# An adaLN attention and MLP block on one core: modulation raws asked for earlier, first MLP weights split earlier, raw tokens kept in SBUF, LayerNorm transposes in the products' bank rotation

## The chip, the cores and the metric

The kernel runs on one core of a Trainium2 chip. The metric is the device time of one execution in microseconds, the median of several runs. The engines are called as in the profile: PE is TensorE, DVE is VectorE, ACT is ScalarE, POOL is GpSimd, SP is SyncE, which here only issues DMAs.

## The reference

One transformer block for 2048 tokens of width D = 576, conditioned on a vector c.

```python
mod = (silu(c) @ w_mod).reshape(6, 576)          # sa, ca, ga, sb, cb, gb
h = layernorm(x) * (1 + ca) + sa
x = x + ga * attention(h)                        # 32 query heads on 16 cached kv heads, head width 128,
                                                 # only the last 512 of the 2048 cached keys, softmax, @ wo
h = layernorm(x) * (1 + cb) + sb
gate, up = h @ W_gate, h @ W_up                  # F = 4608
x = x + gb * ((where(gate > 0, gate, 0) * up) @ W_down)
```

## The kernel before

All matrix products are made in fp32r with operands split into a high and a low part (hi, lo), and a product is three matmuls: hi x hi, hi x lo, lo x hi.

Attention runs in 128 **units**; a unit is one kv group, one block of 512 queries and one of the two heads. On the engines a unit is: scores s (PE, L446 to L448), their row maxima (DVE, L451 to L466), spread over partitions by two small matmuls with the constant quad (PE, L474), mask mb and scaled scores p (DVE, L521), exponentials (ACT, L523), hi (ACT, L510) and lo (POOL, L530), row sums ks (half on DVE, L536, half on POOL, L539), the product with v (pv, PE, L548 to L550), the next unit's queries (qps, PE, L374; qhi on ACT, qlo on DVE, L430) and a piece of the output projection (wo, PE, L575, added up through ACT, L584 and L608). In a unit all these stages belong to different units of a software pipeline.

After the units comes the gated **MLP**. The gate and up products of a pair of F tiles with a half of the tokens are made by a Strassen-like scheme of seven products P1, P6, P2, P7, P5, P4, P3 (gu, L915); P2 is added up in the bank pair of P1 and P3 in that of P5. There are 18 pairs for each of two token halves, m = 0 to 35. After a product, DVE and ACT gate it (L936 to L965), ACT and POOL split the result into hhi (L930) and hlo (L931), and md matmuls (L575) multiply it by W_down; DVE adds md to acc (L586). The operands of the seven products are sums of parts of the tokens (names B11, B21, B22, T1 to T4, h in the code) and of the weights (wop, wk). The sums are made once: `h0_comb` and `h0_cut` make the token operands of the first half from SBUF tiles h0, `h_later(1, ...)` those of the second half, `w_later` the weight operands of the first pair from DRAM. Each such item is a load (begin), one or more combinations (comb), a split into hi and lo (cut) and stores into DRAM (hkeep, wkeep), from which they are loaded when the MLP needs them.

PSUM has a pool psS with two double banks, psW with one, and px["x"] with one in the MLP. In the MLP the gate/up products take psS, psS, x in turn, and md takes psW.

The order of the instructions on PE, DVE, ACT and POOL is written out by hand, and kept. Work that does not belong to the steady pipeline is placed by a table: `step(name, t, fn)` runs fn at t = 10 * unit + position. A unit has four hooks at the positions 0, 4, 6 and 9, and `prep(name, t, pr, gap)` runs the compute part at hook t and issues its load gap hooks earlier. SP's order is that in which the loads are issued; a load waits on SP for its buffer. In the MLP `mat(m, s, fn)` places fn after product s of pair m. `prep_mod(j, t)` loads a raw slab wm of w_mod for row j (L136) into pool xp's tag xm (three buffers, which the ks tiles use too), and multiplies it onto macc (DVE, L126, L128); five slabs make a row; `mod_col(j)` turns it into a column with five small matmuls (mps, L165).

The second LayerNorm is made in two places. `norm_steps("b0"/"b1", ...)` makes token blocks 0 and 1 during the last units; the transposes are ltb (L317), the affine parts lfb (ACT L331, DVE L329), and they are stored as hb in DRAM and loaded again as h0. `ln_half` makes blocks 2 and 3 in the MLP, in pairs m = 2, 4, 6, 8: stats, norm, and three groups of transposes (ltlh, L897) with their affine (lflh, ACT, L900).

```python
        def trans(ds):
            ps = psW.tile([P, 2, 512], F32, tag="w", name=f"lt{nm}_{ds[0]}")
...
    for i in range(4):
        for s, fn in enumerate(ln_half(2 + i // 2, i % 2)):
            mat(2 + 2 * i, s, fn)
```

H in the table is 1070, ten times the number of unit 107.

Of the kernel before, what the change touches and what calls it, by code (L numbers as in the profile page):

```python
# [14 lines left out]
P = 128  # L15
# [18 lines left out]
def kernel(  # L34
# [215 lines left out]

    pend, pend_act = [], []
# [8 lines left out]
    class LayerNorm:  # L260
# [59 lines left out]
        def affine(self, ds, pool, tag, engs):  # L320
            qb = self.qb
            if self.key == "b":
                add, mul = mods["b"]
                for d, e in zip(ds, engs):
# [7 lines left out]
                    hb_store(qb, d, slice(0, 512), f[:n], nc.scalar)  # L332
# [417 lines left out]
    def h_later(b, s, t):  # L750
# [3 lines left out]
        eng = nc.vector if b else nc.gpsimd  # L754
# [15 lines left out]
        def comb(i):  # L770
            x, y = st["a"][:n], st["b"][:n]
            eng.tensor_tensor(x, x, y, op=ALU.add if terms[i][0] == "+" else ALU.subtract)
# [17 lines left out]
        return [begin] + ([cut] if len(terms) == 1 else [lambda i=i: comb(i) for i in range(1, len(terms))])  # L790

    h0 = {}
# [5 lines left out]
    def h0_comb(dst, a, b, t, op):  # L798
        n = 96 if t == 2 else P
        nc.vector.tensor_tensor(h0[(*dst, t)][:n], h0[(*a, t)][:n], h0[(*b, t)][:n], op=op)  # L800
# [22 lines left out]
    def w_later(s, xx, where):  # L823
# [14 lines left out]
        def comb(i):  # L838
            x, y = st["a"], st["b"]
            eng.tensor_tensor(x, x, y, op=ALU.add if terms[i][0] == "+" else ALU.subtract)  # L840
            if i + 1 < len(terms):
                get(st["b"], *terms[i + 1][1:])
            else:
                cut()
# [11 lines left out]
        return [begin] + ([cut] if len(terms) == 1 else [lambda i=i: comb(i) for i in range(1, len(terms))])  # L856

    def ln_half(qb, hh):
# [28 lines left out]
        def trans(ds):  # L887
            ps = psW.tile([P, 2, 512], F32, tag="w", name=f"lt{nm}_{ds[0]}")
            ps = ps.rearrange("p a (b n) -> p (a b) n", b=2)
# [3 lines left out]
            else:  # L893
                f = hp.tile([P, 2, 256], F32, tag="hT", name=f"lf{nm}_{ds[0]}")
# [9 lines left out]
        return [stats, norm, lambda: trans((0, 1)), lambda: trans((2, 3)), lambda: trans((4,))]  # L904
# [39 lines left out]

    def new_pair(m, s):
        i = npair[0]
        npair[0] += 1
        if i % 3 == 2:
            pair[m, s] = px["x"].tile([P, 2, 512], F32, tag="x", name=f"gu{i}")
        else:  # L950
            pair[m, s] = psS.tile([P, 2, 512], F32, tag="s", name=f"gu{i}")
# [146 lines left out]
    for t in range(5):  # L1098
# [11 lines left out]
               (H + 39, H + 39, H + 49, H + 49), (H + 51, H + 61, H + 71), (H + 51, H + 61, H + 71), www)  # L1110
    norm_steps("b1", 1, "b", None, None, (H + 34, H + 37, H + 40, H + 47), H + 48,
               (H + 59, H + 59, H + 69, H + 69), (H + 81, H + 91, H + 101), (H + 81, H + 91, H + 101), www)
# [122 lines left out]
    def then(fn):  # L1235
        def go():
            flush_stores(2)
# [3 lines left out]
    t = 952  # L1241
    items = [(s, xx) for s in ("P1", "P2", "P4", "P7", "P5", "P6", "P3") for xx in range(2)]
    for n, (s, xx) in enumerate(items):
        here = n < 7
        for fn in w_later(s, xx, (xp, "xm", 640) if here else (hp, "hT", 512)):
            step("w.l", t, fn if here else then(fn))
            t += 5 if here else 4
        if here:
            step("w.e", t + 3, flush_stores)
            t = t + 5 if n < 6 else 1062  # L1250
    step("w.e", t + 6, flush_stores)
    t0 = H + 74
    for t in range(3):
        step("h0.l", t0, h0_load, 0, 0, t)
        step("h0.l", t0, h0_load, 1, 0, t)
    cuts = [("B11", (0, 0), t) for t in range(3)] + [("B21", (1, 0), t) for t in range(3)]
    for n, c in enumerate(cuts):
        step("h0.c", t0 + 4 + 4 * n, then(lambda c=c: h0_cut(*c)))
    t0 = H + 104
    seq = []  # L1260
    for t in range(3):
        step("h0.l", t0 + 4 * t, h0_load, 1, 1, t)
        step("h0.l", t0 + 4 * t, h0_load, 0, 1, t)
        seq += [(h0_cut, "B22", (1, 1), t), (h0_comb, (1, 1), (1, 1), (0, 1), t, ALU.subtract),
                (h0_cut, "T3", (1, 1), t), (h0_comb, (1, 1), (1, 1), (0, 0), t, ALU.add),
                (h0_cut, "T2", (1, 1), t)]
    for t in range(3):
        seq += [(h0_comb, (0, 1), (0, 1), (0, 0), t, ALU.subtract), (h0_cut, "T1", (0, 1), t),
                (h0_comb, (1, 0), (1, 0), (1, 1), t, ALU.subtract), (h0_cut, "T4", (1, 0), t)]
    for n, c in enumerate(seq):  # L1270
        step("h0.s", t0 + 6 + 3 * n, then(lambda c=c: c[0](*c[1:])))
    step("h0.e", t0 + 9 + 3 * len(seq), flush_stores)
# [34 lines left out]
    for u in range(NU):  # L1307
# [108 lines left out]
```

## Time and profile before

| | |
|---|---|
| times of three runs | 3138.55, 3129.92, 3129.11 us; median 3129.92 |
| profiled execution | 3133.55 us; span 3131.8, mean granted PE clock 0.974 |
| matmuls and weight loads on PE | 15414 each, PE busy 2949.8 us |
| DMA | 435.82 MB, mean 139 GB/s |
| units 0 to 127 | from about 44 to 1766 us of the span |
| MLP pairs m = 0 to 35 | from about 1766 us to the end |

The page's first part gives the busy time of each engine. A windows view gives the same for chosen stretches, with the clock that PE was granted (1.00 is full). A waits view gives, for an engine and a line, what released it: total wait, how often, the longest. A line view gives the count of instructions, their busy time, mean duration in ns, and the idle time just before them.

### The profile page before, as it was taken

What the parts mean: (1) busy time and instruction counts of PE and PEld (TensorE: products, weight loads), DVE (VectorE), ACT (ScalarE), POOL (GpSimd) and SP (SyncE); (2) the same over time, 40 slices, a digit from 0 to 9 for tenths busy, and PEclk for the clock granted to TensorE, in tenths of its full rate; (3) what the DMA queues carried; (4) which work ended last, traced back from release to release, by engine and by line L of the source; (5) the groups of instructions that cost most, each with busy time, mean ns of one, the idle gap of its engine ahead of it and who ended that gap; (6) DMA issues with size and microseconds to landing.
All of it is one profiled execution on the core that took longest, in us unless ns stands there. A gap on an engine that the chain in (4) does not pass through costs nothing. (4 is left out here: it accounts for less than half of the span.)

```text
span 3131.8 us, 41177 instructions
## 1 busy us (share of the span) xinstructions
PE 2949.8 (94%) x15414; PEld 2544.4 (81%) x15414; DVE 2102.8 (67%) x2925; ACT 1369.8 (44%) x1885; POOL 1848.4 (59%) x1294
## 2 busy tenths in 40 slices
PE   6799999999999999998889988899989999999999
PEld 4688877877888888887777777778778888888888
DVE  7888877877888888776677555556676544444444
ACT  4466665656666666665555333332323211111110
POOL 5578877877788887777677555556666411111111
PEclk8899999999999999999999999999999999999999
DMA  4011122222212203232344555556777954444453
GB/s 143 23 60 52 47 91 80 82 88 91 82 58 81 65 31 107 85 131 80 127 160 146 180 213 212 198 209 234 259 266 261 335 178 173 159 162 165 166 172 113
DMA packets 173447, 435.82 MB, mean 139 GB/s; under 512 B 16128, under 2 KB 62976, under 8 KB 173248
## 3 DMA queue, kind: packets, MB, share of 16 engines
q1 hardware_dynamic: 131344, 291.36, 28.5%
q10 hardware_dynamic: 41904, 141.84, 11.6%
q8 instruction: 122, 2.00, 0.3%
q14 instruction: 77, 0.63, 0.1%
HBM read 283.71 MB, written 177.73 MB: 147 GB/s over the span
## 5 line engine op out<-in xcount | busy, mean ns | idle before, releaser
L530 POOL TENSOR_TENSOR lo<-p,hi 128x1024 fp32r<-128x1024 f32 x256 | 612.6, 2415 | 1.2 <-ACT hi L510 0.9
L539 POOL TENSOR_TENSOR ks<-ks,p 128x512 f32<-128x512 f32 x256 | 343.0, 1340 | 340.0 <-ACT p L523 302.6
L575 PE MATMUL md<-wogb,hhi 128*128 128x288 f32 x2304 | 479.1, 300 | 51.9 <-ACT lflh L900 32.1
L915 PE MATMUL gu<-hop_T,wop 128*128 128x512 f32 (+1 forms) x2016 | 500.5, 393 | 0.0
L586 DVE TENSOR_TENSOR acc<-md,acc 128x576 f32<-128x576 f32 x288 | 217.6, 755 | 420.0 <-PE md L575 419.9
L575 PEld LDWEIGHTS md<-wogb,hhi 128*128 128x128 f32 x2304 | 391.4, 192 | 82.6 <-ACT lflh L900 37.3
L915 PEld LDWEIGHTS gu<-hop_T,wop 128*128 128x128 f32 (+1 forms) x2016 | 369.2, 188 | 67.9
L915 PE MATMUL gu<-hop_B,wop 128*128 128x512 f32 (+1 forms) x1512 | 382.6, 396 | 3.7 <-DMA wop<-wk_P 2.8
L451 DVE TRANSPOSE_TENSOR_REDUCE t<-s 128x32 f32<-128x1024 f32 x256 | 314.8, 1240 | 103.7 <-PE s L448 94.1
L575 PE MATMUL md<-wogb,hlo 128*128 128x288 f32 x1152 | 345.1, 300 | 2.3 <-POOL hlo L931 2.3
L931 POOL TENSOR_TENSOR hlo<-r,hhi 128x512 fp32r<-128x512 f32 x72 | 98.9, 1374 | 408.9 <-issue 242.4
L915 PEld LDWEIGHTS gu<-hop_B,wop 128*128 128x128 f32 (+1 forms) x1512 | 282.0, 191 | 60.6 <-DMA wop<-wk_P 3.3
L374 PE MATMUL qps<-hTa,wA 128*128 128x512 f32 x1288 | 311.8, 393 | 8.5 <-ACT lfa L356 5.2
L575 PE MATMUL wo<-woga,ohi 128*128 128x288 f32 x1472 | 305.9, 300 | 2.3 <-DVE lfa L354 1.6
L374 PEld LDWEIGHTS qps<-hTa,wA 128*128 128x128 f32 x1288 | 244.2, 190 | 61.8 <-ACT lfa L356 5.6
L521 DVE TENSOR_TENSOR p<-s,mb 128x1024 f32<-128x1024 f32 x242 | 285.4, 1218 | 3.4
L523 ACT ACTIVATE p<-p 128x1024 f32<-128x1024 f32 x242 | 255.6, 1056 | 41.9 <-DVE p L521 35.6
L510 ACT CAST hi<-p 128x1024 fp32r<-128x1024 f32 x256 | 268.6, 1049 | 7.0
L575 PEld LDWEIGHTS wo<-woga,ohi 128*128 128x128 f32 x1472 | 238.6, 188 | 10.1 <-issue 2.0
L930 ACT CAST hhi<-r 128x512 fp32r<-128x512 f32 x72 | 44.7, 621 | 431.8 <-DVE r L940 368.3
L426 ACT ACTIVATE qhi<-qps 128x512 fp32r<-128x512 f32 x128 | 76.4, 597 | 350.5 <-PE qps L374 340.5
L575 PEld LDWEIGHTS md<-wogb,hlo 128*128 128x128 f32 x1152 | 220.9, 192 | 3.0 <-POOL hlo L931 3.0
(198 smaller groups left out, 5952.0 us busy)
## 6 DMA issues: line engine op xcount, KB each, us to landing
wop<-wk_P SPq DMA_DIRECT2D x133, 640.0 KB
wk_P<-wop ACTq DMA_DIRECT2D x119, 640.0 KB
wr<-wlay SPq DMA_DIRECT2D x68, 384.0 KB
dk<-wogb ACTq DMA_DIRECT2D x36, 576.0 KB
wogb<-dk SPq DMA_DIRECT2D x36, 576.0 KB
againq<-akq SPq DMA_DIRECT2D x18, 640.0 KB
rogb<-wd SPq DMA_DIRECT2D x36, 288.0 KB
rwA<-wq SPq DMA_DIRECT2D x32, 320.0 KB
```

Of the source, the lines that this page charges most:

```text
L374: return [lambda i=i, a=a, b=b: nc.tensor.matmul(ps, a, b, start=(i == 0), stop=(i == n - 1)) for i, (a, b) in enumerate(ops)]
L426: nc.scalar.activation(qhi[u], qst[u][0], AF.Copy, bias=0.0, scale=SCALE)
L451: nc.vector.tensor_reduce(t4[u][:, 2 * h:2 * h + 2, :].rearrange("p k b -> p (k b)"), t.rearrange("p k (b j) -> p (k b) j", j=32), axis=AX ...
L510: nc.scalar.copy(hi_[u, h], pt[u, h])
L521: nc.vector.tensor_tensor(p, t, bc[u][:, None, :].to_broadcast([P, 2, 512]), op=ALU.subtract)
L523: nc.scalar.activation(p, p, AF.Exp, bias=0.0, scale=1.0)
L530: nc.gpsimd.tensor_sub(lo_[u, h], pt[u, h], hi_[u, h].bitcast(F32))
L539: nc.gpsimd.tensor_tensor(ks_[u], ks_[u], p[:, j, :], op=ALU.add)
L575: nc.tensor.matmul(ps[:, half, :H2], a[:, sl], w[b][:, cs], start=(n == 0 and seed is None), stop=(n == 5), skip_group_check=seed is not None)
L586: nc.vector.tensor_tensor(av, ps[:, :, :H2], av, op=ALU.add)
L915: nc.tensor.matmul(ps, a, c, start=s not in ("P2", "P3") and i == 0, stop=i == len(ops) - 1, skip_group_check=True)
L931: nc.gpsimd.tensor_sub(lo, r, hi.bitcast(F32))
```

## The change

1. Modulation raws: the 15 slabs stand at t = 109 + 30 i instead of 104 + 50 i, and are asked for five hooks ahead instead of two. The columns m3.col and m4.col move from 310 and 560 to 230 and 380. The last row, macc5, is stored in DRAM at 536 and loaded back at 936, ahead of its use at 949, which stays.
2. The first MLP weights' operands (14 items of `w_later`) move from t = 952 and after (seven in the xm buffers, seven in the buffers hT) to units 55 to 90, all in xm. A comb and its cut, one step before, are two steps, 6 apart.
3. The affine results of blocks 0 and 1 are kept as h0 in SBUF for four of five column groups; eight stores (ACT) and eight loads (SP) fall away. The fifth group's two halves are stored by SP at H + 86 and H + 116 and loaded. The subtractions (DVE) and cuts (ACT, POOL) have a new table: cuts at positions 1 and 2 of a unit, subtractions at position 8. Operands' stores go out on SP instead of ACT, with four instead of two left waiting. Normalising and transposes of b0 and b1 move by up to a unit.
4. `ln_half`: stats run in the pair before, at its sixth product, and there are two groups of transposes instead of three: the last 64 columns after product 1, the other 512 after product 5. They take their PSUM from the rotation of the gate/up products (`new_banks`) instead of psW, and their affine result goes to a buffer of pool wC.
5. `h_later(1, ...)`: the combinations run on POOL instead of DVE, cut is a step of its own, and the operands B11 and B21 move to m = 5 to 8.
6. In each unit, `ksum_op` stands after `sum_bc` and `q_lo` instead of ahead of them.

```diff
-                    hb_store(qb, d, slice(0, 512), f[:n], nc.scalar)
+                    if d < 4:
+                        h0[d // 2, qb, d % 2] = f
+                    else:
+                        late.append(lambda f=f: hb_store(qb, 4, slice(0, 512), f[:64]))
...
-    def flush_stores(left=0):
+    def flush_stores(left=0, eng=None):
         while len(stores) > left:
             dst, src = stores.pop(0)
-            nc.scalar.dma_start(dst.bitcast(F32), src.bitcast(F32))
+            (eng or nc.scalar).dma_start(dst.bitcast(F32), src.bitcast(F32))
...
-        eng = nc.vector if b else nc.gpsimd
...
-            eng.tensor_tensor(x, x, y, op=ALU.add if terms[i][0] == "+" else ALU.subtract)
+            nc.gpsimd.tensor_tensor(x, x, y, op=ALU.add if terms[i][0] == "+" else ALU.subtract)
             if i + 1 < len(terms):
                 get(st["b"], *terms[i + 1][1:])
-            else:
-                cut()
...
         def trans(ds):
-            ps = psW.tile([P, 2, 512], F32, tag="w", name=f"lt{nm}_{ds[0]}")
+            ps = new_banks(f"lt{nm}_{ds[0]}").rearrange("p a (b n) -> p (a b) n", b=2)
...
-                f = hp.tile([P, 2, 256], F32, tag="hT", name=f"lf{nm}_{ds[0]}")
+                f = wp.tile([P, 4, 256], F32, tag="wC", name=f"lf{nm}_0")
...
-        return [stats, norm, lambda: trans((0, 1)), lambda: trans((2, 3)), lambda: trans((4,))]
+        return [stats, norm, lambda: trans((4,)), lambda: trans((0, 1, 2, 3))]
...
+    def new_banks(nm):
+        npair[0] += 1
+        pool, tag = (px["x"], "x") if npair[0] % 3 == 0 else (psS, "s")
+        return pool.tile([P, 2, 512], F32, tag=tag, name=nm)
...
-        prep(f"m{3 + i // 5}.{i % 5}", 104 + 50 * i, prep_mod(3 + i // 5, i % 5))
-    step("m3.col", 310, setd(mods, "b0", lambda: mod_col(3, 0.0)()))
-    step("m4.col", 560, setd(mods, "b", lambda: (mods["b0"], mod_col(4, 1.0)())))
+        prep(f"m{3 + i // 5}.{i % 5}", 109 + 30 * i, prep_mod(3 + i // 5, i % 5), 5)
+    step("m3.col", 230, setd(mods, "b0", lambda: mod_col(3, 0.0)()))
+    step("m4.col", 380, setd(mods, "b", lambda: (mods["b0"], mod_col(4, 1.0)())))
...
     for i in range(4):
-        for s, fn in enumerate(ln_half(2 + i // 2, i % 2)):
-            mat(2 + 2 * i, s, fn)
-    later = [fn for s in TERMS for t in range(3) for fn in h_later(1, s, t)]
-    for i, fn in enumerate(later):
+        m = 2 + 2 * i
+        for at_, fn in zip(((m - 1, 5), (m, 0), (m, 1), (m, 5)), ln_half(2 + i // 2, i % 2)):
+            mat(*at_, fn)
+    later = {s: [fn for t in range(3) for fn in h_later(1, s, t)] for s in TERMS}
+    for i, fn in enumerate(later.pop("B11") + later.pop("B21")):
+        mat(5 + i // 3, (0, 2, 4)[i % 3], fn)
+    for i, fn in enumerate(sum(later.values(), [])):
         mat(9 + i // 7, i % 7, fn)
...
-            flush_stores(2)
+            flush_stores(4, nc.sync)
...
-    t = 952
...
+    t = 546
+    for s in ("P1", "P2", "P4", "P7", "P5", "P6", "P3"):
+        for xx in range(2):
+            for fn in w_later(s, xx, (xp, "xm", 640)):
+                step("w.l", t, fn)
+                t += 6
             step("w.e", t + 3, flush_stores)
-            t = t + 5 if n < 6 else 1062
+            t += 6
+    assert t < 930, t
...
         exp_half(u, 1)
-        ksum_op(u, 0)
-        ksum_op(u, 1)
         if u:
             sum_bc(u - 1)
         if u + 1 < NU:
             q_lo(u + 1)
+        ksum_op(u, 0)
+        ksum_op(u, 1)
```

The order on the engines shows the moves at three places. First PE in pair m = 2 of the MLP (ltlh is a transposes' bank, gu a gate/up product's, md the down product's). Before, the transposes stand behind a finished product, and md comes seven matmuls later:

```order
L915 MATMUL gu_17631<-hop_B_2_16570,wop_17626 128x512
L897 MATMUL ltlh_0_0_17786<-ident,xnlh_0_0_17737 128x128
L897 MATMUL ltlh_0_0_17786<-ident,xnlh_0_1_17739 128x128
L915 MATMUL gu_17798<-hop_T_0_16826,wop_17677 128x512 x2
L915 MATMUL gu_17798<-hop_T_3_16829,wop_17677 128x512
L915 MATMUL gu_17798<-hop_T_1_16827,wop_17677 128x512 x2
L915 MATMUL gu_17798<-hop_T_4_16830,wop_17677 128x512
L915 MATMUL gu_17798<-hop_T_2_16828,wop_17677 128x512
L575 MATMUL md_1_0_17806<-wogb_17453,hhi_01_17622 128x288 x2
```

Now the first group there has 64 rows and stands one product earlier, and the others come together four products later:

```order
L916 MATMUL gu_17686<-hop_T_2_16531,wop_17566 128x512
L898 MATMUL ltlh_0_4_17721<-ident,xnlh_0_0_17681 64x128
L898 MATMUL ltlh_0_4_17721<-ident,xnlh_0_1_17683 64x128
L916 MATMUL gu_17625<-hop_B_0_16557,wop_17620 128x512 x2
L916 MATMUL gu_17625<-hop_B_3_16560,wop_17620 128x512
L916 MATMUL gu_17625<-hop_B_1_16558,wop_17620 128x512 x2
L916 MATMUL gu_17625<-hop_B_4_16561,wop_17620 128x512
L916 MATMUL gu_17625<-hop_B_2_16559,wop_17620 128x512
L579 MATMUL md_0_3_17736<-wogb_17433,hhi_00_17423 128x288 x2
```

The neighbours have the same shapes in both; moved are the place of the transposes and the bank that they hold while md comes.

Second, DVE in unit 120 (p are the scaled scores, ks the sums, qlo the next queries' low part, rb the output's scale, h or lfb the raw tokens h0). Before:

```order
L504 STREAM_TRANSPOSE mb_15961<-r_15957 128x512
L800 TENSOR_TENSOR h_111_15622<-h_111_15622,h_001_15138 128x512
L521 TENSOR_TENSOR p_0_15990<-s_0_15915,mb_15961 128x1024
L521 TENSOR_TENSOR p_1_15995<-s_1_15924,mb_15961 128x1024
L536 TENSOR_TENSOR ks_15998<-p_0_15990 128x512
L484 STREAM_TRANSPOSE rb_16002<-ri_15959 128x512
L430 SCALAR_TENSOR_TENSOR qlo_16004<-qps_15941,qhi_15963 128x512
L556 TENSOR_TENSOR rb_16002<-pv_15980,rb_16002 128x512
L451 TENSOR_REDUCE t_121_16052<-s_0_16045 128x32
```

After:

```order
L508 STREAM_TRANSPOSE mb_15932<-r_15928 128x512
L525 TENSOR_TENSOR p_0_15958<-s_0_15878,mb_15932 128x1024
L525 TENSOR_TENSOR p_1_15963<-s_1_15887,mb_15932 128x1024
L488 STREAM_TRANSPOSE rb_15966<-ri_15930 128x512
L434 SCALAR_TENSOR_TENSOR qlo_15968<-qps_15906,qhi_15934 128x512
L540 TENSOR_TENSOR ks_15970<-p_0_15958 128x512
L560 TENSOR_TENSOR rb_15966<-pv_15948,rb_15966 128x512
L804 TENSOR_TENSOR lfb_2_15487<-lfb_2_15487,lfb_0_14942 128x512
L804 TENSOR_TENSOR lfb_3_15489<-lfb_3_15489,lfb_1_14944 128x512
L804 TENSOR_TENSOR lfb_0_15353<-lfb_0_15353,lfb_0_14942 128x512
L804 TENSOR_TENSOR lfb_1_15355<-lfb_1_15355,lfb_1_14944 128x512
L455 TENSOR_REDUCE t_121_16015<-s_0_16008 128x32
```

The subtraction has left its place ahead of p, four stand in a row at the unit's end, and ks has gone behind qlo.

Third, the combinations of `h_later` in the MLP (hx is the operand in the making, acc the sum of md, hlo the low part that md needs, wop weights' operands). Before they stand on DVE, in the first pairs that have several terms, between the acc additions:

```order
L772 TENSOR_TENSOR hx_T_0_20618<-hx_T_0_20618 128x512
L586 TENSOR_TENSOR acc_125<-md_0_0_20672,acc_125 128x576
L586 TENSOR_TENSOR acc_126<-md_0_1_20693,acc_126 128x576
L730 TENSOR_TENSOR wr_01_20516<-wr_01_20516,wr_00_20379 128x768
L772 TENSOR_TENSOR hx_T_0_20618<-hx_T_0_20618 128x512
L586 TENSOR_TENSOR acc_127<-md_0_2_20735,acc_127 128x576
```

Now they stand on POOL, between hlo and the weights:

```order
L775 TENSOR_TENSOR hx_T_0_20063<-hx_T_0_20063 128x512
L932 TENSOR_TENSOR hlo_00_20137<-r_20133,hhi_00_20136 128x512
L695 TENSOR_TENSOR wop_20140<-wr_11_19803,wop_20140 32x2x128
L696 TENSOR_TENSOR wop_20140<-wr_11_19803,wop_20140 128x2x256
L177 TENSOR_TENSOR wogb_20146<-rogb_20061,wogb_20146 128x576
L775 TENSOR_TENSOR hx_T_0_20063<-hx_T_0_20063 128x512
L695 TENSOR_TENSOR wop_20184<-wr_01_19848,wop_20184 32x2x128
```

The number of matmuls is the same in both programs.

More of the change, by code (lines that the diff above doesn't have):

```diff
@@ L249, in hb_load @@
             nc.sync.dma_start(dst[:96], hb[qb, 4][j].rearrange("r p n -> (r p) n"))
+    h0, late = {}, []
     pend, pend_act = [], []
@@ L788, in cut @@
             stores.append((hkeep[b, s, t], hi[:n]))
-        return [begin] + ([cut] if len(terms) == 1 else [lambda i=i: comb(i) for i in range(1, len(terms))])
-    h0 = {}
+        return [begin] + [lambda i=i: comb(i) for i in range(1, len(terms))] + [cut]
+    H0_COMB = {"t3": ((1, 1), (1, 1), (0, 1), ALU.subtract), "t2": ((1, 1), (1, 1), (0, 0), ALU.add),
+               "t1": ((0, 1), (0, 1), (0, 0), ALU.subtract), "t4": ((1, 0), (1, 0), (1, 1), ALU.subtract)}
+    H0_CUT = {"B11": (0, 0), "B21": (1, 0), "B22": (1, 1), "T3": (1, 1), "T2": (1, 1), "T1": (0, 1),
+              "T4": (1, 0)}
     def h0_load(j, k, t):
@@ L854, in cut @@
             stores.append((wkeep[0, s][:, xx, 3:5, :].rearrange("p t n -> p (t n)"), lo))
-        return [begin] + ([cut] if len(terms) == 1 else [lambda i=i: comb(i) for i in range(1, len(terms))])
+        return [begin] + [lambda i=i: comb(i) for i in range(1, len(terms))] + [cut]
     def ln_half(qb, hh):
@@ L1251 @@
[L1251 to L1272, printed above, removed]
+    t = 546
[4 more added lines that the diff above has]
+                t += 6
+            step("w.e", t + 3, flush_stores)
+            t += 6
@@ L1273 @@
+    assert t < 930, t
+    for key, t, at_ in [(("l", 0, 0), 2, 96), (("l", 1, 0), 2, 96), (("l", 1, 1), 2, 122), (("l", 0, 1), 2, 122),
[7 rows of a table added]
+        if key[0] == "l":
+            step("h0.l", H + at_, h0_load, *key[1:], t)
+        elif key in H0_COMB:
+            step("h0.a", H + at_, h0_comb, *H0_COMB[key], t)
+        else:
+            step("h0.c", H + at_, then(lambda key=key, t=t: h0_cut(key, H0_CUT[key], t)))
+    step("h0.e", H + 181, flush_stores, 0, nc.sync)
     for t, s in ((1236, "B11"), (1246, "T2"), (1247, "B21"), (1266, "T3"), (1267, "T1"), (1276, "T4"),
```

31 lines of the change are left out of this document (12 added, 19 removed), and 7 rows, old and new, of the table t.

## The prediction

> **What bounds the kernel now.** I read the page's busy shares first, then windows laid over single units and single MLP pairs, then the waits inside the long ones, then the tiles and lines that the change moves.
>
> ```profile
> PE 2949.8 (94%) x15414; PEld 2544.4 (81%) x15414; DVE 2102.8 (67%) x2925; ACT 1369.8 (44%) x1885; POOL 1848.4 (59%) x1294
> ```
>
> TensorE (PE) is the bound and the others have room, so only time in which PE idles or runs slowly can be won. In the next fence each window is one unit, from its spread matmuls (L474) to the next unit's; or one or several pairs m of the MLP; the columns are PE, weight loads, DVE, ACT, POOL, granted clock, DMA share, GB/s.
>
> ```profile
> 453.60:476.80 23.20, 16.24 (x76) 13.97 (x75) 11.24 (x17) 7.68 (x10) 13.10 (x8) 0.78 0.21 70
> 476.80:488.90 12.10, 12.10 (x66) 10.57 (x65) 9.44 (x14) 8.77 (x12) 6.83 (x5) 1.00 0.22 71
> 526.50:547.10 20.60, 15.05 (x64) 12.34 (x65) 11.35 (x16) 8.73 (x12) 11.46 (x8) 0.83 0.33 111
> 658.40:677.70 19.30, 14.84 (x65) 11.95 (x65) 10.15 (x15) 8.83 (x12) 11.48 (x7) 0.82 0.33 117
> 726.20:745.60 19.40, 14.66 (x66) 11.99 (x65) 11.65 (x16) 7.68 (x10) 13.06 (x8) 0.82 0.34 119
> 794.70:813.60 18.90, 16.59 (x75) 13.96 (x74) 13.01 (x17) 8.83 (x12) 14.78 (x9) 0.82 0.21 69
> 1439.80:1748.60 308.80, 267.66 (x1316) 224.20 (x1314) 217.56 (x328) 173.52 (x241) 224.91 (x155) 0.94 0.43 142
> 1812.60:1847.90 35.30, 35.30 (x196) 31.21 (x195) 24.08 (x34) 12.33 (x17) 24.21 (x24) 1.00 0.61 221
> 1847.90:1894.70 46.80, 38.79 (x205) 33.41 (x204) 22.87 (x28) 12.97 (x20) 22.00 (x20) 0.96 0.55 193
> ...
> 2094.00:2140.60 46.60, 38.56 (x206) 33.27 (x204) 22.86 (x28) 13.48 (x21) 22.96 (x21) 0.96 0.57 199
> 2140.60:2419.60 279.00, 257.81 (x1359) 223.23 (x1358) 189.68 (x211) 85.15 (x125) 182.86 (x160) 0.97 0.75 263
> 1040.00:1366.00 326.00, 325.10 (x1707) 280.11 (x1706) 264.00 (x382) 214.62 (x286) 256.78 (x157) 1.00 0.24 79
> ```
>
> An undisturbed unit takes 12.1 us, an undisturbed pair 35.3. Against these floors there are four pools of lost time. A: units 30, 35, 45, 50, 55, together 101.4, less 5 x 12.1, is 40.9. B: the 20 units from 107 on, 308.8 less 242, is 66.8. C: pairs m = 2, 4, 6, 8 (first and last shown, 186.8 in all) less 141.2, is 45.6. D: seven pairs from m = 9, 279.0 less 247.1, is 31.9. Between 1040 and 1366 PE is 99.7% busy, so outside the pools little is left.
>
> **A: modulation raws.**
>
> ```profile
>   DMA wm<-wmod: 24.3, 4
> 450.33 5.47 SPq L136 DMA_DIRECT2D wm<-wmod  x1
> 461.83 0.82 DVE L128 SCALAR_TENSOR_TENSOR macc<-wm,sT,macc 128x576 f32<-128x576 f32 x1 [6.83 <-DMA wm<-wmod]
> DVE roga L217 <- DMA roga<-wo: 0.9, 1, 0.9
> SPq L136 <- DVE t L466: 18.3, 3, 6.6
> ```
>
> DVE waited 24.3 us in four waits for raws, and PE idles 101.4 - 77.4 = 24.0 in the five windows: the same microseconds, since the q_lo behind macc on DVE is what PE needs. The other 17 are half clock: 0.82 of 18.9 us is 3.4 lost. The raw of unit 30 was issued at 450.3, the issue alone took 5.5, and macc began only at 461.8: 11.5 later, and about 15 after the hook that asked for it (an estimate: one position of the unit more). There are four hooks to a unit of 12.1: two ahead are 6 us, five 15.7. Four waits should go. The m.col steps remain (now at units 23 and 38, directly behind the last raw's macc): unit 55 had no raw wait and still lost 6.8, so I leave 2 x 7. Gain 40.9 - 14 = 27 (18 if one or two raws stay late, 35 if the columns cost little). The parked macc5 is one store on ACT and one load on SP, the load a unit ahead of its use; by L136's 5.5 at most such an issue is nothing against the 24.3 that PE felt, and in the stretch of the load SP has room: 0 (to 5, if the load is late like a raw).
>
> **B: the last units.** Three things leave or spread here: 14 weight items, eight stores and eight loads of raw tokens, and the bunching of subtractions and cuts.
>
> ```profile
> ACT wb_P L849 <- POOL wa_P L840: 35.6, 7, 7.2
> PE qm L474 <- DVE t L466: 14.7, 5, 4.7
> PE wo L575 <- ACT wo L608: 14.6, 10, 4.1
> PE s L448 <- DVE qlo L430: 6.0, 6, 2.3
> DVE h L800 <- POOL hz_T L808: 7.0, 2, 3.5
> SPq L830 <- POOL wa_P L840: 58.3, 6, 19.1
> L800 DVE TENSOR_TENSOR h<-h,h 128x512 f32<-128x512 f32 x8 | 12.0, 1501 | 8.1 <-POOL hz_T L808 7.0 <-POOL hz_B L808 1.2
> L317 PE MATMUL ltb<-ident,xnb 128*128 128x128 f32 x32 | 4.1, 272 | 0.0
> L840 POOL TENSOR_TENSOR wa_P<-wa_P,wb_P 128x384 f32<-128x384 f32 x13 | 13.2, 1012 | 5.6 <-DMA wb_P<-wlay 3.0 <-DVE ri L479 2.5
> ```
>
> ACT stood 35.6 us for the weight combination in front of its own cut (both in one step), and PE's wait for the wo copy, 14.6, is ACT being late. That goes with the weights, as far as ACT caused it. DVE stood 7.0 for POOL inside a unit; with cuts and subtractions in different places of the unit that goes too. What stays: 40 LayerNorm transposes on PE (4.1 busy for 32, so 5), the LayerNorm's own DVE work, and 12 subtractions (h0). Four of them now stand in a row at the end of unit 120, three in 121: at 0.7 (L772's fastest, below) to 1.5 each, 2.8 to 6.0 us where DVE has (326 - 264) / 27 = 2.3 of room per unit. The sum of the pool: PE idle is 308.8 - 267.7 = 41.1, of which the three PE rows are 35.3; slow clock is 0.06 of 308.8, 18.5; transposes and the rest 7. Afterwards the wo wait leaves 2, the qm wait 8 (DVE's work is only spread), the s wait 3, the unnamed 6: idle 19, slow clock in the same ratio 9, transposes and the rest 7: 35 (20 to 50). Gain 66.8 - 35 = 32 (17 to 47). The 21 operand stores go from ACT to SP, flushed with four left; an SP store holds what is queued behind it until POOL's cut has ended. Before, SP stood 58.3 us for POOL in this stretch and PE waited for no DMA, so I cost it at 0; without that cover (holds over 19 us) the `again` loads come late.
>
> The weights' new place, units 55 to 90, has POOL 256.8 busy of 326, so 2.6 idle per unit; it receives 14 combinations of 1.01 and 14 cuts (taken as long again), about 30 us into 35 units, or 0.9 per unit. It fits on average; a unit that gets both has 2.0 more where 2.6 are free. I take 8 lost for all 35 units (0 to 25).
>
> **C: LayerNorm transposes inside the MLP.**
>
> ```profile
> PE md L575 <- ACT lflh L900: 32.1, 12, 4.2
> 1847.68 0.60 PE L897 MATMUL ltlh<-ident,xnlh 128*128 128x128 f32 x4
> 1852.22 0.53 PE L575 MATMUL md<-wogb,hhi 128*128 128x288 f32 x2 [2.32 <-ACT lflh L900]
> 1864.24 0.69 DVE L940 SCALAR_TENSOR_TENSOR c<-c,gu 128x512 f32<-128x512 f32 x1
> 1868.15 0.56 ACT L900 ACTIVATE lflh<-ltlh,mcol,mcol 64x256 f32<-64x256 f32 x1
> 1868.76 0.85 PE L575 MATMUL md<-wogb,hhi 128*128 128x288 f32 x2 [4.16 <-ACT lflh L900]
> ```
>
> The transposes stood in md's only bank, so md waited for ACT's affine (lflh): 12 waits, 32.1. Ten transposes a pair, at 0.60 for four, are 1.5, in all 6; slow clock (0.04 of 186.8) is 7: together the 45.6. Afterwards md does not meet them. They take a turn in the three banks of the gate/up products. By that rotation the 64-row transposes take a free bank, and the next product waits only for one affine, a whole product (35.3 / 7 = 5.0) after them: no wait. The 512-row ones at position 5 push the next pair's first product onto the bank that the last product has just filled; it must wait for its three DVE steps like L940 (0.7 each, with their start 2.2). So per pair 1.5 of transposes, 2.2 of wait, 0.8 for the four affines in a row in front of hhi on ACT: 4.5, 18 in all. Gain 45.6 - 18 = 28 (15 to 36).
>
> Whether the 2.2 us also slows the clock is open. The Trainium skill, page "TensorE: Matmul & The Clock Gate", section "Why this matters for your kernels", asks only for no idle gaps over about 3 us; by that the four waits cost nothing more, and C stays at 28. This trace disagrees: unit 55 idles 2.3 us in all and its clock is 0.82, 3.4 us lost. By that row C would be 28 - 4 x 3.4 = 14; pair m = 2 had the gap of 2.32 as well as that of 4.16, and lost only 0.04 of 46.8, 1.9, at both, so I keep 28 and let 15 stand as the end.
>
> **D: second half of the raw tokens' operands.**
>
> ```profile
> PE md L575 <- DVE acc L586: 18.6, 9, 5.2
> DVE hx_T L772 <- DMA hx_T<-hb: 16.4, 6, 4.7
> L772 DVE TENSOR_TENSOR hx_T<-hx_T x21: 679/890/2480, 2205.7 to 2383.5; 128x512 f32<-128x512 f32 x14, 96x512 f32<-96x512 f32 x7
> L575 PE MATMUL md<-wogb,hlo 128*128 128x288 f32 x268 | 81.7, 305 | 0.9 <-POOL hlo L931 0.9
> L784 POOL TENSOR_TENSOR hx_T<-hx_T,hy_T x8: 1267/1286/1295, 2213.7 to 2367.0; 128x512 fp32r<-128x512 f32 x8
> ```
>
> DVE waits for token loads (16.4) while md's accumulation stands behind it, and PE waits 18.6 for that. The 21 combinations go to POOL: by L784 about 1.29 each, 27 us into 279 - 183 = 96 of idle. The DMA waits go with them, and there hlo stands behind, which md needs too. PE waited for hlo only 0.9 here, with POOL's 1.3 us operations already between, so hlo has room, how much no row tells. B11 and B21 move to m = 5 to 8, where DMA is at 0.57 instead of 0.75. I let half go: 16 (0 if the waits only change engine, 27 if hlo's room takes them).
>
> **Unit order.** ks of the probabilities now follows q_lo. It saves the 0.7 that DVE stands for ACT ahead of ks, and one ks.
>
> ```profile
> DVE ks L536 <- ACT p L523: 64.4, 86, 1.4
> PE s L448 <- DVE qlo L430: 13.6, 19, 2.3
> ```
>
> PE's 13.6 fall by some 5 outside pool A; ks ends no later than POOL's half. With the 8 lost above: -3.
>
> **Sum.** 27 + 32 + 28 + 16 - 3 = 100. The profiled execution took 3133.55 (span 3131.8 and 1.75 around it); 3133.55 - 100 = 3033.5. The median of the runs, 3129.92, lies 3.6 under it, so about 3030.
>
> **Rivals.**
> First, the tail's stalls only change place: four subtractions in a row on DVE in unit 120, and POOL instead of DVE standing for token loads. For it speaks that DVE's L800 takes 1501 ns on average where L772 can take 679, against it that ACT's 35.6 go anyway. B gains 10 and D nothing: 27 + 10 + 28 - 3 = 62, 3068. Chance 0.2.
> Second, all lands: A 38, B 45, C 36, D 25, order and weights +3: 147, 2983. Every pool would have to reach nearly its floor, against the 40 transposes and two columns that stay. Chance 0.09.
> Third, the change does not do what it says in A: raws still late, since five hooks (15.7) barely cover the 15 of unit 30. A gains 5: total 78, 3052. Against it: of the weights, asked four to six hooks ahead, only one wait for a load shows in all units (roga, 0.9). Chance 0.06, within the range.
> Fourth, slower: raws asked earlier hold SP. A raw's load waits for the buffer that the previous ks leaves (18.3 in three waits before, 6.6 at most), and all weight loads queue behind it. At 6.7 us lost per raw, 15 x 6.7 = 100, the whole gain is gone; with 10 it is 3130 + 50 = 3180. Against it: the buffer is freed by the same unit's L466, before the hook that now asks; before, holds of 6.6 made no unit late. Chance 0.09.
>
> **How the numbers follow.** The forecast has 0.56. Its own range: half the width of each term's ends (8.5, 15, 10.5, 13.5, and 12.5 for unit order and weights), squared, added, and the root taken, is 27: 3003 to 3057. To leave no more than 2 in 10 out, the range goes to 2988, at the second case, and to 3078, past the first. This measurement tells about 0.3%, 9 us, from no change. All cases but the fourth lie over 9 us below 3130: faster 0.91; the fourth's 0.09 is 0.03 within 0.3% (at its turning point) and 0.06 slower.
>
> **What the changed profile would show.** A: no DVE wait for wm, units 30 to 55 at 12.1, two dips at units 23 and 38. B: no PE wait for the wo copy; the units from 107 on at 277 for 20; PE waits for qm at unit 121 if the row of four hurts. C: no md wait for lflh, pairs 2 to 8 at 39.8, each followed by one wait of gu for DVE's L941. D: md waits for hlo instead of acc, less than half as long. The forecast is wrong if the 35 units from 55 on lose over 25, if PE waits for a load, or if the 2.2 us waits in C bring the clock down.

## The result, and the profile after

The changed kernel takes 3047.33 us (median of four, 3045.8 to 3051.58) against 3129.52 before: ratio 0.9734, 95% interval 0.9713 to 0.9755. It is 82 us faster; 100 were forecast, with a range of 2988 to 3078. The profiled execution took 3047.34, span 3045.6, 86.2 under the span before.

The page's first part after, and the same windows as before laid on the same units and pairs (PE, weight loads, DVE, ACT, POOL, granted clock, DMA share, GB/s). In order: units 10 to 54, unit 22 with the column m3.col, unit 55, units 56 to 106, the 20 units from 107, unit 120, then pairs 1, 2, 5, 6, and the seven pairs from 9. (A window of a pair runs, before and after, from the pair's fourth product to the next pair's.)

```profile
PE 2912.7 (96%) x15414; PEld 2531.2 (83%) x15414; DVE 2087.4 (69%) x2904; ACT 1369.5 (45%) x1885; POOL 1873.0 (61%) x1315
```
```profile
200.80:759.70 558.90, 551.54 (x2901) 478.56 (x2900) 455.01 (x664) 371.70 (x497) 460.25 (x274) 0.99 0.25 83
345.90:361.90 16.00, 15.27 (x75) 12.90 (x74) 11.37 (x17) 7.62 (x10) 13.29 (x8) 0.89 0.17 52
759.70:780.30 20.60, 14.20 (x65) 12.20 (x64) 9.55 (x14) 8.99 (x13) 12.00 (x9) 0.83 0.30 101
780.30:1410.60 630.30, 621.80 (x3270) 538.87 (x3269) 501.81 (x728) 416.65 (x559) 518.22 (x332) 1.00 0.26 85
1410.60:1685.90 275.30, 254.56 (x1316) 217.57 (x1314) 219.94 (x328) 171.46 (x233) 207.17 (x130) 0.97 0.41 135
1579.20:1598.50 19.30, 12.24 (x65) 10.37 (x64) 18.77 (x18) 9.41 (x13) 18.45 (x11) 0.89 0.28 102
1749.80:1787.10 37.30, 35.81 (x198) 31.27 (x197) 24.19 (x34) 12.68 (x18) 24.35 (x24) 1.00 0.60 217
1787.10:1827.20 40.10, 37.75 (x203) 33.02 (x202) 23.64 (x27) 12.51 (x19) 22.71 (x20) 0.96 0.67 240
1904.80:1944.70 39.90, 37.27 (x196) 32.33 (x194) 25.26 (x33) 13.13 (x19) 26.37 (x26) 0.96 0.57 203
1944.70:1987.10 42.40, 38.31 (x204) 33.50 (x205) 24.53 (x28) 13.49 (x21) 23.98 (x21) 0.96 0.69 249
2069.10:2336.20 267.10, 254.06 (x1359) 220.58 (x1359) 181.25 (x189) 82.24 (x120) 199.92 (x173) 0.99 0.73 255
```

For comparison, the same for units 10 to 54 and 56 to 106 of the kernel before:

```profile
204.60:794.70 590.10, 562.42 (x2892) 479.85 (x2891) 461.99 (x656) 371.95 (x497) 461.02 (x274) 0.97 0.23 76
813.60:1439.80 626.20, 623.26 (x3270) 536.09 (x3269) 509.70 (x733) 414.17 (x553) 498.53 (x306) 1.00 0.25 81
```

Units 10 to 54 won 31.2, and unit 55 is 1.7 longer for a new reason. Units 56 to 106, which took the weights, lost 4.1. The last units won 33.5, although unit 120 takes 19.3. Pairs 2, 4, 6, 8 came down, but pairs 1, 3, 5, 7, at 35.3 before, take 37.3 to 39.9: over the eight pairs only 8.7 were won. The seven pairs from 9 won 11.9. Some 4 us each were won at the start and in pair 17.

The waits answer to those of before, in four fences: 150 to 1440 us, the last units, pairs 0 to 8, pairs 9 to 15. Columns are total, times, longest.

```profile
DVE t L455 <- PE s L452: 125.9, 88, 3.2
ACT wb_P L851 <- DMA wa_P<-wlay: 11.2, 1, 11.2
PE wo L579 <- ACT wo L612: 6.4, 1, 6.4
DVE roga L217 <- DMA roga<-wo: 9.6, 5, 2.3
DVE ks L540 <- ACT p L527: 3.2, 3, 2.0
```
```profile
PE qm L478 <- DVE t L470: 11.2, 5, 7.1
PE wo L579 <- ACT wo L612: 4.2, 6, 0.7
```
```profile
PE gu L916 <- ACT lflh L901: 12.7, 6, 3.2
PE md L579 <- DVE acc L590: 8.2, 4, 2.6
```
```profile
PE md L579 <- DVE acc L590: 11.2, 7, 2.7
POOL hx_T L775 <- DMA hx_T<-hb: 6.5, 5, 2.2
```

No wait for a raw is left. The wait for the wo copy, 14.6 at the end before, is 4.2. In the MLP md no longer waits for the LayerNorm's affine, but gu does, and md for acc.

### The profile page after: what moved, and what is told of

It is laid out like the page before. It is cut to its first block, busy times and chain, and to the rows that moved or that the text cites. A ratio compares the mean times of both kernels' runs of the same rounds, so it can differ in the third digit from the quotient of the medians.

```text
span 3045.6 us, 41170 instructions
## 1 busy us (share of the span) xinstructions
PE 2912.7 (96%) x15414; PEld 2531.2 (83%) x15414; DVE 2087.4 (69%) x2904; ACT 1369.5 (45%) x1885; POOL 1873.0 (61%) x1315
## 3 DMA queue, kind: packets, MB, share of 16 engines
q10 hardware_dynamic: 35632, 130.53, 10.9%
## 5 line engine op out<-in xcount | busy, mean ns | idle before, releaser
L916 PEld LDWEIGHTS gu<-hop_B,wop 128*128 128x128 f32 (+1 forms) x1512 | 281.9, 191 | 71.5 <-ACT lflh L901 12.7
L579 PE MATMUL wo<-woga,olo 128*128 128x288 f32 x736 | 219.2, 298 | 7.2 <-POOL olo L568 7.2
```

The source lines that it names most:

```text
L579: nc.tensor.matmul(ps[:, half, :H2], a[:, sl], w[b][:, cs], start=(n == 0 and seed is None), stop=(n == 5), skip_group_check=seed is not None)
L916: nc.tensor.matmul(ps, a, c, start=s not in ("P2", "P3") and i == 0, stop=i == len(ops) - 1, skip_group_check=True)
```

## The experiments

All are edits of the changed kernel, except the last two. Medians are of four runs.

**Lead of the raws.**

```diff
-        prep(..., 109 + 30 * i, prep_mod(3 + i // 5, i % 5), 5)
+        prep(..., 109 + 30 * i, prep_mod(3 + i // 5, i % 5), 2)
```

> Changed kernel with the modulation raws asked two hooks ahead again, at their new places (every third unit). Theory: the lead is what pool A was lost for. The raws of some four to seven of units 10 to 53 then land late again in the stretch from 380 to 760 us, DVE waits for wm 15 to 35 us, and with half clock 25 to 55 us come back: 3072 to 3102. Rival: the earlier places (before most weight copies) are what helped, and the lead nothing: no wait for wm above 3 us, 3045 to 3050.

3069.02. Who waited for the raws' tile:

```profile
  DMA wm<-wmod: 34.8, 9
```

Nine raws come late, and units 10 to 54 take 29 more. Unit 55 is 7.9 shorter beside that, and the total lies 3 below the range. The theory holds: the lead counts, the new places alone do not help.

**Banks of the MLP.** `new_banks` takes the bank that was released longest ago (`free_banks` notes when a pair's last reader, or a transposes' affine, has been issued), and the statistics move:

```diff
-        pool, tag = (px["x"], "x") if npair[0] % 3 == 0 else (psS, "s")
+        tag = min((v[0], k) for k, v in freed.items() if v)[1]
+        freed[tag].pop(0)
...
-        for at_, fn in zip(((m - 1, 5), (m, 0), (m, 1), (m, 5)), ln_half(...)):
+        for at_, fn in zip(((m - 1, (6, 6, 2, 2)[i]), (m, 0), (m, 1), (m, 5)), ln_half(...)):
```

> Changed kernel in which gate/up products and LayerNorm transposes take the bank that was released longest ago, instead of every third from x, and in which the LayerNorm statistics stand after product 7 of the pair before (halves 1, 2) or after its product 3 (halves 3, 4), instead of after its product 6. Theory: the waits of the next pair's first product (2.35 to 3.2 us, four times) come from the bank rotation, each with a clock dip of 1.7, and the 2.0 us lost in pairs 1 and 3 come from 2.1 us of statistics on DVE ahead of acc. Pairs 1 and 3 then take 35.3 instead of 37.3, pairs 2 and 4 about 37 instead of 40.2, pairs 5 to 8 lose 4 us less each where they carry token operands too: 3047 - 22 = 3025 (3018 to 3032). Rival: the wait of the first product is for the four affines on ACT, whatever the bank: only the statistics' 8 us go, 3039.

3022.43. Pairs 1, 2, 7 and 8 by windows:

```profile
1746.90:1783.70 36.80, 35.80 (x197) 31.27 (x197) 25.49 (x33) 12.67 (x18) 24.40 (x24) 1.00 0.64 225
1783.70:1819.90 36.20, 36.20 (x203) 32.07 (x203) 22.22 (x28) 12.51 (x19) 23.15 (x20) 1.00 0.66 237
1967.60:2006.10 38.50, 36.20 (x197) 31.13 (x197) 27.73 (x34) 13.12 (x19) 25.49 (x26) 1.00 0.65 230
2006.10:2042.30 36.20, 36.20 (x203) 32.07 (x202) 23.15 (x27) 13.41 (x21) 25.28 (x23) 1.00 0.80 276
```

Pair 8 is at pair 2's value. With other banks PE does not idle in pairs 2 and 8 at all, and the clock stays at 1.00, though the four affines still stand in a row on ACT: the wait was for the bank, and the affine that the waits view names only ended beside DVE's gating. The statistics are only in part answered: after the last product of pair 1 they still cost md 1.0, so pair 1 is 36.8 and not 35.3, and at their earlier place in pairs 5 and 7 md waits 1.84, so pair 7 takes 38.5. In all 25 us go, 23.9 of them in pairs 1 to 8, as the theory says; the run changes the banks and the statistics together, and only the windows tell their shares apart. (The expectation counts products by place: its 7 is P3, its 3 is P2, its 6 is P4.)

**B11 and B21 later.**

```diff
-    for i, fn in enumerate(later.pop("B11") + later.pop("B21")):
-        mat(5 + i // 3, (0, 2, 4)[i % 3], fn)
     for i, fn in enumerate(sum(later.values(), [])):
-        mat(9 + i // 7, i % 7, fn)
+        mat(9 + i // 8, min(i % 8, 6), fn)
```

> Changed kernel with the operands B11 and B21 of the second half made in pairs 9 to 16 (eight steps to a pair) instead of pairs 5 to 8. Theory: these items, not the LayerNorm, make pairs 5 to 8 2.4 us longer each than pairs 1 to 4; so pairs 5 to 8 become 37.3, 40.2, 37.3, 40.2 (10 us less), and pairs 9 to 16, which lose 20 us in the changed kernel, lose 5 to 15 more, since they carry 63 steps instead of 51: 3042 to 3052. Rival: pairs 5 to 8 are longer for another reason (transfers are denser there: DMA share 0.67 to 0.69) and stay at 39.9 and 42.2: 3052 to 3062.

3051.46. Pairs 5 to 8, then 9 to 16, of this kernel, and below them of the changed one:

```profile
1904.90:2058.50 153.60, 145.95 (x797) 127.77 (x796) 96.36 (x121) 50.91 (x75) 94.85 (x89) 0.99 0.62 219
2058.50:2373.90 315.40, 294.81 (x1553) 255.00 (x1552) 215.16 (x217) 95.58 (x140) 232.58 (x201) 0.97 0.75 261
```
```profile
1904.80:2069.10 164.30, 151.07 (x797) 131.67 (x796) 100.11 (x120) 53.23 (x80) 101.92 (x95) 0.96 0.64 229
2069.10:2371.80 302.70, 289.62 (x1553) 251.74 (x1553) 204.02 (x216) 92.81 (x135) 225.00 (x195) 0.99 0.75 259
```

10.7 go in the one stretch and 12.7 come in the other. The theory holds: each stretch pays for these items, and the move is worth some 2 us in these windows (4 by the medians).

**Combinations on DVE.**

```diff
-            nc.gpsimd.tensor_tensor(x, x, y, op=ALU.add if terms[i][0] == "+" else ALU.subtract)
+            nc.vector.tensor_tensor(x, x, y, op=ALU.add if terms[i][0] == "+" else ALU.subtract)
```

> Changed kernel with the combinations of the second half's token operands on DVE again; places unchanged. Theory: the move of the 21 combinations to POOL is worth the 11.6 us that pairs 9 to 16 won; on DVE PE waits for acc behind token loads again, 8 to 16 us more: 3055 to 3064. Rival: pairs 9 to 16 won because they carry 12 steps less and DVE or POOL is the same: 3045 to 3050, and DVE's waits for token loads are absorbed.

3061.60; pairs 9 to 16:

```profile
2065.30:2382.30 317.00, 293.19 (x1553) 254.15 (x1553) 217.06 (x237) 92.53 (x135) 197.30 (x175) 0.97 0.71 248
```
```profile
PE md L579 <- DVE acc L590: 23.3, 13, 4.1
DVE hx_T L775 <- DMA hx_T<-hb: 15.5, 11, 2.3
```

14.3 come back, all of D and more; the theory holds.

**Subtractions spread, and subtractions on POOL.** In the first, units 119 to 123 get 2, 2, 3, 3, 2 of the 12 instead of 2, 4, 3, 2, 1:

```diff
-  ("t2", 0, 138), ("t2", 1, 138), ("t1", 0, 138), ("t1", 1, 138), ... ("t3", 2, 148), ("t4", 0, 148), ("t4", 1, 148)
+  ("t2", 0, 138), ("t2", 1, 138), ... ("t3", 2, 148), ("t1", 0, 148), ("t1", 1, 148), ... ("t4", 0, 158), ("t4", 1, 158)
```

The last subtraction of T1 moves from unit 122 to 123, and three cuts of T1 and T4 move with their subtractions.

> Changed kernel with the 12 subtractions of the raw tokens (h0) spread two or three to a unit over units 119 to 123, instead of 2, 4, 3, 2, 1. Theory: unit 120 and 121 lose 7.2 and 3.7 us because four subtractions in a row, 2.2 us each beside POOL's lo, hold the next maxima; spread, these two units lose 3 to 5 together and the others 1 to 3 more: 3047 - 5 = 3042 (3039 to 3046). Rival: each subtraction costs PE its 2 us wherever it stands: unchanged, 3045 to 3050.

3038.30. In the second only the engine changes, `nc.gpsimd.tensor_tensor` in `h0_comb`:

> Changed kernel with the 12 subtractions of the raw tokens on POOL, at the same places. Theory: on DVE they are slow because POOL's lo reads SBUF at the same time; on POOL they take 1.3 us each, but POOL has 207 of 275 us busy in units 107 to 126 and its lo is then 5 us late in unit 120: units 120 and 121 lose 3 to 8 instead of 11: 3040 to 3047. Rival: the count of operations at one place decides, whichever engine: 3046 to 3052.

3048.46. The line of the subtractions in the changed kernel, spread, and on POOL:

```profile
L804 DVE TENSOR_TENSOR lfb<-lfb,lfb x8: 681/1786/2879, 1573.2 to 1609.0; 128x512 f32<-128x512 f32 x8
```
```profile
L804 DVE TENSOR_TENSOR lfb<-lfb,lfb x8: 678/1776/1785, 1572.7 to 1615.7; 128x512 f32<-128x512 f32 x8
```
```profile
L804 POOL TENSOR_TENSOR lfb<-lfb,lfb x8: 1277/1290/1299, 1573.9 to 1608.3; 128x512 f32<-128x512 f32 x8
```

And unit 120 with the subtractions spread, to be held against 19.3 above:

```profile
1578.70:1592.50 13.80, 12.25 (x65) 10.39 (x64) 13.23 (x16) 9.41 (x13) 13.03 (x8) 1.00 0.33 115
```

The spread wins 9, slightly more than its theory allowed. Units 119 to 123 give 8.5 of it: unit 120 5.5, where the row of four is gone, and unit 123 3.1, where PE waited 3.0 for POOL's olo and where the edit also changes the cuts. On POOL a subtraction is shorter but nothing is won: unit 120 takes 12.9, but unit 121 20.5, since four in a row hold POOL 5.0 us ahead of its lo, and unit 123, where PE waits 3.8 for POOL's olo, 20.6. Theory of the first and rival of the second hold: for unit 120 the row of four is the fault, whichever engine it stands on; in unit 123 PE waits for POOL.

**Weights ahead of ks.** All steps of `w_later` at position 5 of successive units from 55 on, the first load 11 positions ahead of its cut.

```diff
-            for fn in w_later(s, xx, (xp, "xm", 640)):
-                step("w.l", t, fn)
-                t += 6
+            step("w.l", t - 6 if t == 550 else t - 1, fns[0])
+            for fn in fns[1:]:
+                t += 5 if fn is fns[1] else 10
+                step("w.l", t, fn)
```

> Changed kernel with the combinations and cuts of the first MLP weights at position 5 of successive units from 55 on (right ahead of POOL's ks, where POOL waits for ACT some 2 us in each unit), and the first load 1.1 units ahead of its cut instead of 0.6. Theory: the 8.5 us of unit 55 are the first load, asked too late, and some 4 to 8 us of units 56 to 106 are POOL's items that fall where POOL is needed; both go: 3047 - 13 = 3034 (3031 to 3038). Rival: POOL's total is what counts, not the place: only unit 55 changes, 3038 to 3042.

3035.81. Unit 55, then unit 56 and units 57 to 106:

```profile
757.40:769.50 12.10, 12.10 (x65) 10.56 (x65) 9.34 (x14) 9.19 (x13) 10.65 (x8) 1.00 0.27 92
769.50:785.80 16.30, 12.27 (x66) 10.38 (x64) 11.95 (x15) 8.73 (x12) 11.37 (x10) 1.00 0.39 126
785.80:1398.20 612.40, 609.51 (x3205) 529.44 (x3206) 496.16 (x713) 408.25 (x547) 512.16 (x324) 1.00 0.26 85
```

Inside the theory's range. All 8.5 of unit 55 go, which was the late load, but unit 56, at 12.1 in the changed kernel, now loses 4.2: ACT stands 3.7 there for the second load, which is still asked only six positions ahead, and DVE 3.8 in front of roga, for which PE waits 4.0. Units 57 to 106 took 618.2 and win 5.8, so the items' place on POOL was felt as the theory says. What is left of the loads' lateness is in unit 56.

**Old unit order.**

```diff
+        ksum_op(u, 0)
+        ksum_op(u, 1)
         if u:
             sum_bc(u - 1)
         if u + 1 < NU:
             q_lo(u + 1)
-        ksum_op(u, 0)
-        ksum_op(u, 1)
```

> Changed kernel with ksum_op ahead of sum_bc and q_lo again. Theory: the new order saved 3 to 9 us, mostly single units of 12.3 to 13.3 us before unit 55 and some in units 56 to 106: 3050 to 3056. Rival: it saved nothing that PE felt: 3045 to 3049, and DVE waits 0.7 for ACT ahead of ks in each unit without a longer unit.

3074.46: 27 us, three times the theory's upper end, so neither theory nor rival. Units 10 to 54, unit 22 of them, and units 56 to 106:

```profile
199.30:775.50 576.20, 559.51 (x2902) 480.06 (x2901) 473.48 (x664) 371.50 (x497) 464.84 (x274) 0.99 0.24 80
348.50:367.50 19.00, 16.74 (x76) 14.05 (x75) 12.22 (x17) 7.62 (x10) 13.42 (x8) 0.82 0.16 44
796.00:1434.00 638.00, 626.69 (x3270) 536.42 (x3269) 513.33 (x728) 416.48 (x559) 519.90 (x332) 1.00 0.26 84
```
```profile
DVE ks L540 <- ACT p L527: 84.5, 102, 7.6
DVE t L455 <- PE s L452: 60.4, 66, 2.6
```

With ks in front, DVE stands 84.5 us for ACT in the middle of the unit and 60.4 for PE at its end; with ks behind, 3.2 and 125.9. Units 10 to 54 lose 17 and units 56 to 106 8 without the new order.

In the two long windows DVE's idle time is nearly the same (window less busy time: 227 us here, 232 in the changed kernel). Its busy time is not: 473.5 and 513.3 here against 455.0 and 501.8, 30 us more for the same number of instructions. The raws' macc and roga, which makes the wo weights, show where most of it lies, first in this kernel, then in the changed one:

```profile
L128 DVE SCALAR_TENSOR_TENSOR macc<-wm,sT,macc x12: 1261/1579/1846, 244.3 to 745.8; 128x576 f32<-128x576 f32 x12
L217 DVE TENSOR_TENSOR roga<-roga,mrow x32: 734/1586/2946, 67.8 to 1232.8; 128x576 f32<-128x576 f32 x32
```
```profile
L128 DVE SCALAR_TENSOR_TENSOR macc<-wm,sT,macc x12: 803/807/1853, 243.1 to 729.5; 128x576 f32<-128x576 f32 x12
L217 DVE TENSOR_TENSOR roga<-roga,mrow x32: 743/749/1846, 67.7 to 1209.8; 128x576 f32<-128x576 f32 x32
```

The medians (the middle numbers, in ns) halve. So there are two readings, and no run separates them: idle time at the unit's end is room that a macc or a column can take, while in the middle it is not; or these operations, at their new times, run shorter by themselves. The busy time that goes, 30, is more than the 25 that these units win, so the second reading can't be left out.

**The order alone, and the lead alone, in the kernel before.**

> Kernel before with one edit: ksum_op after sum_bc and q_lo. Theory: in the changed kernel this order alone is worth 27 us; it works on every unit, so the kernel before gains about the same: 3130 - 25 = 3105 (3098 to 3112). Rival: the order only pays where the changed kernel put more work into the units (weights in 55 to 90), and gains under 10 here: 3120 to 3130.

3116.75, ratio 0.9956 (0.9938 to 0.9973): 14 us, between the two theories. DVE's two waits turn as above (ks 3.8, t 129.5), and units 10 to 54 and 56 to 106 win 6 each. DVE's busy time falls here too, by 9.3 and 13.9 in the two windows, and the median of roga from 1586 to 749 ns. In the changed kernel the same order is worth twice that; why is not shown.

> Kernel before with one edit: the modulation raws asked five hooks ahead, at their old places. Theory: the four raw waits (24 us) and the half clock behind them (14) go, the two columns stay: 3130 - 34 = 3096 (3092 to 3106). Rival: with the old order of the units the five slabs' macc on DVE cost PE part of it anyway, as in the changed kernel with the old order, where units 10 to 54 won only 14 against before: 3110 to 3118.

3102.32, ratio 0.9913 (0.9895 to 0.9932). Units 10 to 54 win 28 by the edit `..., i % 5), 5)` at the old places:

```profile
200.90:763.40 562.50, 553.00 (x2892) 472.82 (x2891) 463.03 (x656) 372.06 (x497) 462.87 (x274) 1.00 0.24 79
```

The theory holds. With the old order the old places are the better ones: 562.5 against 576.2 with the new places. But one of the two columns stands in unit 55 here and in these units there. Over units 10 to 55, which hold both columns in both kernels, it is 580.0 against 596.7, of which 8.4 is the late load in unit 55, so the new places cost some 8. Whether the new order takes that away is open, since no run has it with the old places and the lead of five.

**Mended together.** Banks by release with the statistics after product 7 (position 3), subtractions spread, weights ahead of ks:

> Changed kernel with three parts mended together: banks by release (as in the run on the bank rotation, statistics now after product 7 of the pair before for all four halves), the 12 subtractions spread, and the weight items at position 5 with the first load earlier. Theory: the three lie in different stretches and add: 3047 - 24 - 9 - 11 = 3003 (2996 to 3010). Rival: what one gains another gives back (transfers at the start of the MLP come denser): 3010 to 3025.

(Product 7 is P7 here, the fourth.)
3008.33 (3006.78 to 3010.79), ratio to the kernel before 0.9611 (0.9597 to 0.9626), 39 under the changed kernel. By themselves the three won 25, 9 and 11.5, so 6 of their sum are missing; the result lies in the theory's range, and the rival's is not reached. It is the fastest version run.

## Why the prediction was right, and where not

| term | forecast | measured | shown by |
|---|---|---|---|
| A, units 10 to 54, and the 6.8 that unit 55 lost before | 27 | 38 | lead undone: 29 back; order undone: 17 |
| B, last units | 32 | 33 | window |
| C, pairs 1 to 8 | 28 | 9 | banks and statistics: 24 more to be had |
| D, pairs 9 to 16 | 16 | 12 | combinations on DVE: 14 back |
| order and weights, units 55 to 106 | -3 | -13 | late load: 8.5; the rest by windows |
| start and pair 17 | 0 | 7 | windows |

The total came this near in part by luck: of the 19 that C and the 10 that order and weights fell short, A paid back 11, and the start and pair 17, which were in no sum, 7.

A: the step holds, raws asked 1.3 units ahead are in time. The columns were put at 2 x 7; with the old order unit 22 does lose 6.9, with the new one 3.9. That the order carries part of A, 17 us, was not seen; without it A would be 21.

B: the sum holds to 1.5 us, and so do its parts: idle 20.7 where 19 was put, wo wait 4.2 for 2, qm wait 11.2 for 8. The row of four was mis-sized: at 0.7 to 1.5 each it was put at 2.8 to 6.0, and it took 8.7. The first rival's row of four came true in this (units 120 and 121 are 10.9 over the floor), but the rest of the pool gave that back, so B did not fall to its 10.

C is the step that failed, and it is the sum that was too short, not its mechanism. Pairs 2 and 4 took 40.1 and 40.3 where 39.8 was forecast, with one wait of 2.35 for DVE's gating where 2.2 was. Two things were left out. The statistics were moved to the pair before, and a moved step's own cost was not counted: 2.1 us of DVE ahead of acc, 2.0 in each of four pairs, 8 in all. The items of B11 and B21 got a place with a DMA share but no price: 10.7 over pairs 5 to 8. A third was weighed and put at nothing: the clock went down after each of the four waits, about 1.6 each, which was one of the prediction's own signs of being wrong. In pairs 2 and 4 it hardly shows in the sum, because the ten transposes cost 0.9 (pair 2 takes 36.2 with other banks) where 1.5 was put, and the 0.8 put down for the affines did not come. The page "TensorE: Matmul & The Clock Gate" of the Trainium skill, section "Why this matters for your kernels", with its gaps over about 3 us, was not a safe limit here: pair 2 idles 40.1 - 37.75 = 2.35 in one gap and shows 0.96, and with the gap gone 1.00. The row of unit 55 gave the right sign, but at 3.4 twice the size; and in the kernel before, the gap of 2.32 in each of the four pairs had no half clock behind it, so 2.3 is no limit either.

D: the mechanism holds in the main. DVE's 16.4 of waits for tokens became 6.5 on POOL; PE's wait for acc fell from 18.6 to 11.2. It is still acc that md waits for, though, and not hlo, as the prediction had it. The two undoings, 14.3 for the combinations and 12.7 for the items of B11 and B21, are together more than D won; what took the rest is open.

Order and weights: the term was two errors in opposite directions. The order was sized at 5, as the sum of PE waits that it removes; undone it costs 27, of which 17 are in A's units; besides the waits it changes DVE's busy time by 30, and how the two share the gain is open. The weights were put at 8 and cost more: 8.5 in unit 55, and units 56 to 106 take 630.3 where the kernel before with the order alone takes 620.1. In unit 55 the first load was asked 0.6 units ahead, in the stretch in which the prediction itself counted 11.5 from issue to landing for a raw. ACT stood 11.2 for it with the wo copy behind. The test that was made for the raws was not made for the loads that the change adds. This was another of the prediction's signs of being wrong, a wait for a load that PE feels.

The fourth rival (SP held by raws) did not come: no wait for a raw is left, and of the weights only roga's loads come later, 9.6 us of DVE in five waits where it was 0.9.

## What to carry to other kernels

When a step moves, price the step at its new place, and ask of each load that moves with it whether its lead covers the latency measured in that stretch. After a change of order compare an engine's busy time as well as its waits: moving one operation that waits in the middle of a period to its end was worth 14 and 27 us here, and other operations, untouched, ran in half the time. When shared buffers rotate by count, an extra user shifts who follows whom; choose the buffer by its release.

## What the runs showed of the hardware

The same subtraction of two SBUF tiles takes 0.68 us on DVE at its fastest, 1.78 as a rule where it stands beside POOL's work, and up to 2.88, while on POOL it takes 1.28 to 1.30 always; four in a row took 8.7 us. The Trainium skill's page "SBUF — State Buffer", section "Who interferes with whom", says that a DVE instruction with two SBUF inputs contends with a GpSimd instruction that reads SBUF; the rows agree. The macc and roga rows, 0.81 against 1.58 and 0.75 against 1.59 us, show the same two speeds; that POOL is the reason there too is likely but not tested.

In pairs 2 to 8 of the changed kernel idle gaps of PE of 2.33 to 3.20 us, the four waits and two for acc, were each followed by one 3.4 us stretch of half clock, six times in six, and gaps of up to 1.5 us were not. Gaps of 1.84 in the run with other banks and of 2.32 in pairs 2, 4, 6, 8 of the kernel before had none behind them, so the length of a gap alone does not decide. In the changed kernel's trace the half-clock stretches begin whole multiples of 3.413 us apart (among others at 355.1, 624.7, 768.1 and 1809.2 us), so where a gap falls may count as well; no run tests that.
